# Two-stage recurrence and feed-forward block on one core: a new order of all steps, and masked copies that run along the groups

## Chip, cores and metric

The kernel runs on one core of one Trainium2 chip. The metric is device time in microseconds of one execution of the program, shown as the median of repeated runs. The core has five engines with instruction streams of their own: PE (TensorE, matrix products), DVE (VectorE), ACT (ScalarE), POOL (GpSimd) and SP (SyncE, which here only issues transfers). Each works its stream strictly in order, and waits on semaphores for the others.

## Reference

The first half is a recurrence over 768 time steps for 4 x 8 heads with a state of 40 x 40 each; the second is a gated feed-forward block on the 3072 tokens of 320 features that come out.

```python
for t in range(S):                       # r, k, v, w, a, b: (4, 8, 768, 40)
    y[:, :, t] = einsum('bhd,bhde->bhe', r_t, state)
    Sa = einsum('bhde,bhe->bhd', state, a_t)
    state = state * w_t[:, :, None, :] - einsum('bhd,bhe->bhde', Sa, b_t)
    state = state + einsum('bhd,bhe->bhde', v_t, k_t)
x = y.transpose(0, 2, 1, 3).reshape(3072, 320)
xn = x / sqrt(mean(x * x) + 1e-6) * rms_g
g = xn @ w_gate                          # 320 x 1536
out = (g * sigmoid(g) * (xn @ w_val)) @ w_out
```

All of it is float32 at the surface; the weights arrive as 64-bit floats and are narrowed on the chip.

## The kernel before

Time is cut into 24 chunks of 32 steps. For each chunk c the kernel records four stages, and for each pair of chunks a fifth:

- `front(c)` (L706) loads w, a, k, b and v of the chunk (POOL issues these transfers from the second chunk on), turns them with TensorE, and builds the strictly lower triangular matrix LT of each of the 32 heads and two halves, 32 x 32. Its entries come from products with a doubling scheme in five levels of block length 1, 2, 4, 8, 16. The innermost blocks of four steps are done at once: one set of 32 small products ("gramk", L551) of K with A gives, for each group of four columns, seven places in PSUM: three for the first diagonal below the main one (distance 1), then two for distance 2 and one that stays unused, then one for distance 3. Three masked copies, one for each distance, put them into LT. For levels 4, 8 and 16 another product and one masked copy each follow, with the mask `msk`. Between the levels VectorE and ScalarE scale and reorder K and A.
- `inverse(c)` (L810) sends LT through DRAM (sB) into the layout M, runs 31 steps of substitution on VectorE (`tmp` and `Yi`, two instructions a step), and sends the result back through DRAM (sY) into LT. SP issues these transfers.
- `main(c)` (L830) uses the inverse: solves for the chunk (X, U, written into VU), updates the state ST, forms the scores As and adds the levels to y; then normalizes and turns the tokens into xg.
- `feed(g)` (L952), after every second chunk, runs the feed-forward block on 256 tokens: 12 slices of the hidden size, whose weights come from DRAM (sW into wf, SP), with products into `ps` and `po`, silu on ScalarE (sg), a product on VectorE (hT).
- `narrow_slice(f)` (L1010) turns the 64-bit weights into float32, once, during the first feed.

The stages only record steps ("pieces"). Each piece has an engine, a time from a formula, and what it reads and writes. What comes out in the program is set by two long tables of numbers at the top of the file. ORDER names the pieces in the order in which they are issued; each engine's stream is that order restricted to its own pieces. Its numbers count from the first piece not yet issued, so that 0 is the oldest open one. A "-" in it issues one filler: a 128 x 128 product of the identity into an unused part of `po` (L1030), which keeps TensorE busy where it would have nothing to do. PAIRS names, for each of 491 uses of PSUM, which of three pairs of banks (ps0 to ps2) it takes. Both tables were written by a search outside this file that uses the pieces' time formulas; the constants S0, S1, LEAD and WARM belong to it. All pieces of one use of a PSUM pair must be done before the next use of the same pair begins.

The time formulas stand in the helpers. For VectorE (L505), a fixed part and 0.00104 us an element; for the masked copy (L519):

```python
def where(o, m, a, more=0.0):
    dve(0.08, nc.vector.copy_predicated, o, m, a, more=more)
```

so that the formula of a masked copy is 0.08 + `more` + 0.00104 for each element of a partition. The formula has no part in the program other than through the order that was searched with it. All VectorE work recorded by these helpers shows line L505 in the profile, ScalarE's copies L532 and activations L528, transfers L548, products L551, turns L554.

The names in the changed lines: LT is (128, 16, 32), a row of 32 columns for each of 16 items; `g j` splits these columns into 8 groups of 4. `near` holds three masks of 32 columns, one for each distance, the same for all items. `g4` is the PSUM result, (128, 16, 8, 7), 64 words from item to item and 7 from group to group.

Of the kernel before, what the change touches and what calls it, by code (L numbers as in the profile page):

```python
# [9 lines left out]
U32 = mybir.dt.uint32  # L10
# [6 lines left out]
P = 128  # L17
# [15 lines left out]
37 346 26 36 42 27 193 38 4 40 16 41 18 39 31 194 28 5 30 19 29 20 46 14 9 50 49 47 192 45 48 33 61 184 66 182 53 51  # L33
54 196 65 21 60 59 - 55 62 8 592 56 25 591 57 186 605 64 181 76 77 63 628 75 191 74 73 58 604 110 22 78 71 - - - - -
- - - - 67 72 602 86 70 603 23 593 34 68 84 85 626 88 82 89 183 - 79 615 594 90 97 185 616 87 83 595 345 201 6 96 32
195 596 265 43 95 11 94 202 629 388 203 35 216 197 204 597 81 99 221 400 606 598 80 391 98 617 - - - - - - - - - 91
69 599 390 208 618 187 205 209 93 399 600 619 389 108 92 601 220 206 15 101 347 620 627 12 219 109 102 214 336 215
100 188 349 210 103 398 217 651 233 397 218 44 227 211 337 387 607 225 402 621 107 226 622 7 245 1128 229 608 630
392 106 212 230 401 105 232 609 242 104 13 348 623 3 610 639 213 611 231 640 - - - - - - - - - - - - - - - - - - 222
350 631 241 228 624 632 223 239 243 253 - 234 612 240 244 238 252 407 111 633 112 237 410 408 113 613 409 114 422  # L40
614 224 235 625 115 251 249 - - - - - 246 650 250 414 236 652 116 52 411 675 1 117 199 118 263 415 412 247 198 119
256 427 120 24 641 421 416 255 121 426 189 258 264 122 439 123 962 674 420 653 10 124 424 257 200 125 423 434 664
417 973 663 126 963 127 435 128 190 129 431 261 130 425 1129 131 436 132 642 418 133 248 419 134 432 - - - - - - - -
- - - - - - - - - - - - 428 438 135 136 634 137 635 444 138 446 139 207 433 140 395 429 141 437 396 142 450 449 - -
- - - - - - 440 445 143 405 447 144 443 406 145 654 457 146 643 441 147 442 636 - 452 148 655 637 456 149 656 150
453 151 462 413 464 152 677 153 154 260 155 156 644 638 463 157 645 262 158 657 676 159 160 259 161 162 461 658 163
164 165 665 166 666 167 168 169 646 451 170 171 266 667 172 267 173 647 659 174 268 254 269 430 455 175 465 454 270
660 271 272 273 668 176 274 669 275 670 648 276 649 671 177 277 278 672 178 179 279 280 180 281 282 714 283 284 712
285 678 711 286 679 287 673 288 - - - - - - - - - - - - - - - - - - - - - - - - - - - - - - - - - - - - - - - - - -
- - - - - - - - - - - - - - - - - - - - - - - - - - - - - 338 289 680 467 290 661 469 0 339 289 466 679 337 686 290  # L50
456 711 291 340 685 292 698 293 680 660 294 681 338 699 295 682 - - - - - - - - - - 341 296 683 349 342 297 723 468
298 540 299 401 464 300 350 301 684 364 351 302 542 722 979 353 15 303 304 713 978 305 714 458 306 307 970 446 308
361 352 309 715 356 310 355 311 357 312 313 354 314 700 - - - - - - - - - - - - - 362 315 724 363 316 365 317 725
318 366 541 319 701 367 320 359 565 543 321 358 469 322 370 702 716 726 323 717 975 470 324 457 727 969 718 371 567
974 471 325 703 327 965 472 0 34 636 393 2 - - - - - - - - - 43 646 0 399 39 391 635 400 144 634 43 239 644 44 145
45 639 146 46 0 374 - - - - - - 650 429 146 375 147 46 430 148 376 654 651 400 653 652 149 377 47 150 378 657 48 151
665 3 655 656 417 152 658 391 153 669 - - - - - - 659 0 153 669 48 667 49 679 678 154 848 663 659 680 71 155 662 61
156 157 665 847 158 660 840 159 160 857 661 161 839 681 162 677 666 60 163 676 - - - - - - - - - - - - - - - - - -
670 400 849 675 164 50 440 850 165 674 1 166 858 430 0 635 380 116 391 642 640 0 116 389 380 637 117 619 349 118 620
381 387 119 661 621 120 635 382 121 - - - - - - - - - - - - - - 161 383 633 122 638 630 163 162 640 123 165 164 636  # L60
124 631 125 632 391 642 126 384 392 127 0 384 392 127 642 128 643 651 393 385 129 394 - - - - 167 653 130 395 0 521
0 515 33 36 518 0 263 0 32 37 263 610 0 39 263 0 43 520 609 521 0 40 518 0 34 298 0 37 298 0 33 514 0 34 - - - - - -
- - 41 0 36 38 0 590 47 0 41 654 42 0 293 643 0 41 293 653 0 514 - - - 41 44 293 599 642 22 498 45 653 0 514 45 2 41
642 22 599 0 433 497 514 582 0 43 442 290 581 640 44 513 291 655 650 583 514 45 292 493 0 45 655 1088 292 506 46 669
656 514 47 293 48 657 507 3 658 661 931 2 515 49 662 674 0 49 515 658 516 50 0 620 466 558 0 345 368 567 512 522 517
369 516 0 369 530 370 518 371 512 528 6 372 513 5 373 514 374 508 431 7 460 375 777 8 0 433 375 434 787 431 376 0
431 776 0 42 528 375 516 441 376 45 0 376 138 377 519 341 441 378 522 379 523 525 528 444 380 536 530 381 529 520
382 521 457 0 442 534 378 445 379 0 500 343 0 402 0 341 401 387 9 342 407 886 343 408 406 449 344 388 410 720 345
738 403 397 346 404 721 347 0 417 397 449 347 412 0 347 9 732 412 348 0 412 732 348 492 413 493 730 349 0 413 235
349 0 484 434 481 349 350 225 414 351 8 488 719 483 485 501 352 720 487 415 7 0 352 54 481 725 353 415 12 716 0 7  # L70
495 725 353 496 415 10 0 715 415 490 0 346 347 32 409 348 31 0 409 484 485 43 0 407 345 38 480 0 345 407 488 484 485
724 408 0 37 569 408 50 719 724 486 725 494 720 345 918 346 27 0 694 319 381 704 882 693 0 898 11 381 20 697 12 538
319 705 322 0 381 538 320 697 465 319 0 697 11 458 0 456 707 0 704 10 537 559 715 718 700 0 17 10 0 10 17 701 0 0
445 6 688 27 682 698 26 699 696 7 305 691 703 683 29 702 28 0 683 0 692 - - - - - - - - 685 689 31 704 708 32 540 3
44 706 687 22 300 703 686 438 2 23 700 436 0 706 700 434 696 3 714 23 41 4 32 300 701 0 692 708 39 707 19 28 293 706
703 292 29 436 37 437 20 693 50 438 0 9 684 418 419 0 682 698 419 692 420 9 488 27 0 9 420 17 489 18 421 0 487 489
490 39 697 421 38 422 9 18 0 413 0 678 - - - - - - - - - - - - 16 8 40 413 0 0 470 404 667 666 0 404 405 27 11 406 0
27 406 29 6 17 407 668 18 469 5 19 408 0 10 651 408 6 38 19 11 0 462 13 44 0 13 401 31 21 0 585 458 10 298 11 18 461
584 398 12 0 18 806 734 39 0 779 18 379 446 776 638 444 439 8 17 575 0 8 29 767 379 30 439 0 447 637 0 - 710 439 7
711 378 440 8 447 713 379 0 456 444 448 8 778 379 9 0 775 379 0 431 769 7 0 757 7 432 755 8 370 440 756 371 - - - -  # L80
- - - - 17 438 0 765 371 0 0 748 8 363 431 753 18 364 13 365 0 365 0 430 432 365 8 366 367 431 0 367 764 368 0 368 5
0 425 757 362 601 363 426 3 600 4 364 365 427 8 690 0 438 427 365 0 0 685 361 423 362 746 363 434 364 686 0 362 745
363 421 585 749 597 0 743 683 1027 745 363 421 757 762 0 363 421 773 748 364 0 421 753 0 421 363 422 2 364 747 753
365 758 3 423 366 755 4 757 367 424 594 0 747 594 367 424 369 755 368 694 766 764 4 370 765 748 0 762 764 590 591
744 0 591 756 365 592 593 594 744 421 0 756 594 595 752 795 368 432 426 753 367 596 754 366 597 761 427 767 365 428
598 769 431 599 770 764 429 773 600 601 421 602 766 603 604 605 765 422 423 768 774 606 607 776 608 609 424 433 777
610 778 785 611 612 787 434 613 690 788 614 615 786 425 436 616 1165 617 618 771 619 430 620 621 790 622 623 440 3
624 792 435 445 444 660 437 457 625 0 625 438 662 626 790 627 660 663 788 437 771 628 440 661 629 441 664 774 457
630 631 632 672 665 633 442 673 726 717 674 780 727 688 676 998 675 997 445 681 716 684 1005 634 446 635 516 636 637
683 447 638 448 639 783 640 679 452 678 677 451 641 680 642 643 682 685 453 644 795 687 449 690 695 691 645 694 692  # L90
# [333 lines left out]
def kernel(  # L424
# [42 lines left out]
    NI = 2 * N  # L467
# [51 lines left out]
    def where(o, m, a, more=0.0):  # L519
        dve(0.08, nc.vector.copy_predicated, o, m, a, more=more)  # L520
# [63 lines left out]
    near = const.tile([P, 3, C], FP32, name="near")  # L584
# [19 lines left out]
    for p0, kt, src in ((0, 0, 0), (0, 1, P), (0, 2, 2 * P), (64, 2, 2 * P)):  # L604
        m = min(P, DM - src)
# [100 lines left out]
    def front(c):  # L706
# [5 lines left out]
        for i in range(2):  # L712
# [6 lines left out]
            for x in range(2):  # L719
                at = i * 64 + x * C  # L720
# [27 lines left out]
        for dist, at in ((1, 0), (2, 3), (3, 6)):  # L748
            m = 4 - dist
# [314 lines left out]
```

## Time and profile before

| what | value |
|---|---|
| median of three runs | 1142.45 us (1137.5, 1142.45, 1143.51) |
| profiled execution | 1136.66 us |
| its span, first to last instruction | 1134.9 us |
| mean granted TensorE clock | 0.976 |
| instructions | 53027 |
| moved by DMA | 145.41 MB, mean 128 GB/s |
| instruction queue q8 | 182 packets, 2.98 MB |

The profile is one execution. PE and PEld are the two parts of TensorE's work, the products and the loads of their stationary operand; each float32 product counts as two passes, so that 275 fillers show as 550. "Idle before" a group is the time in which its engine did nothing just before an instruction of the group, with what ended it; "issue" there means that nothing in the profile explains the wait. The chain is followed from the last instruction back, at each step to what released it. By windows of 100 us, VectorE is busiest between 100 and 200 us (93.6 us of 100), TensorE from 1000 us on (128 of 135).

### The profile page before, as it was taken

The numbers are of one execution on the slowest core, as the hardware profiler recorded it, in microseconds if no ns is written. First come the engines' busy times: TensorE is split into PE (matmuls) and PEld (weight loads), VectorE is DVE, ScalarE is ACT, GpSimd is POOL, SyncE is SP. The second block draws the span as 40 slices with busy tenths as digits, with TensorE's granted clock in tenths as the row PEclk, the third lists the DMA queues.
The fourth block names the chain that finished last, engine by engine and source line by source line (L and its number), as shares of the span: only waits on it lengthen the run. The fifth ranks groups of instructions, "written<-read, shape, count | busy, mean of one in ns | idle before, by whom it ended". The sixth has DMA issues, their size and how long they took to land.

```text
span 1134.9 us, 53027 instructions
## 1 busy us (share of the span) xinstructions
PE 1036.8 (91%) x23142; PEld 853.2 (75%) x23142; DVE 864.5 (76%) x3065; ACT 437.8 (39%) x989; POOL 303.9 (27%) x534
## 2 busy tenths in 40 slices
PE   5988888889999999989998898998999999999998
PEld 4887767767777787767776687877777777777876
DVE  6998998877778789587697588887788787787421
ACT  5644455633433344234333244333334244332211
POOL 8503333221340330511422324213303402401000
PEclk8999999989999999999998999999999999999999
DMA  6645546846454453633644536455445645534342
GB/s 134 173 109 153 139 94 166 236 138 162 115 125 122 128 129 98 141 103 84 150 118 99 136 82 159 113 145 143 110 115 131 147 116 129 148 91 141 87 138 78
DMA packets 171175, 145.41 MB, mean 128 GB/s; under 512 B 123712, under 2 KB 142080, under 8 KB 170944
## 3 DMA queue, kind: packets, MB, share of 16 engines
q1 hardware_dynamic: 152576, 119.06, 38.4%
q0 software_dynamic: 16192, 22.64, 9.7%
q8 instruction: 182, 2.98, 1.1%
q10 hardware_dynamic: 2176, 0.33, 0.2%
q14 instruction: 49, 0.40, 0.1%
HBM read 125.83 MB, written 16.12 MB: 125 GB/s over the span
## 4 chain that ended last, share of the span: by engine, by line
PE 55%; DVE 19%; DMA 10%; issue 6%; SPq 4%; POOL 3%; ACT 2%; DVEq 0%; ACTq 0%; POOLq 0%
PE ps L551 37%; PE po L551 9%; PE ps L554 7%; SPq L548 4%; DVE LT L505 3%; DMA M<-sB 2%; DVE Yi L505 2%; DVE tmp L505 2%; DMA wf<-sW 2%; DVE K L505 2%; PE po L1030 1%; POOL kbn L548 1%; DMA sY<-Yi 1%; DVE Ab L505 1%; DMA sB<-LT 1%
## 5 line engine op out<-in xcount | busy, mean ns | idle before, releaser
L551 PE MATMUL ps<-xg,wf 128*128 128x256 f32 (+1 forms) x1728 | 369.2, 401 | 7.6 <-DMA wf<-sW 2.0
L551 PEld LDWEIGHTS ps<-xg,wf 128*128 128x128 f32 (+1 forms) x1728 | 264.9, 193 | 67.9 <-issue 18.6
L505 DVE TENSOR_TENSOR tmp<-Yi,M 128x60 f32<-128x60 f32 (+24 forms) x744 | 154.3, 208 | 38.0 <-DMA M<-sB 26.5
L551 PE MATMUL po<-wf,hT 128*128 128x320 f32 x576 | 178.6, 440 | 2.0 <-DVE hT L505 1.7
L505 DVE TENSOR_TENSOR Yi<-Yi,tmp 128x60 f32<-128x60 f32 (+24 forms) x744 | 153.9, 208 | 11.9
L551 PEld LDWEIGHTS po<-wf,hT 128*128 128x128 f32 x576 | 104.4, 192 | 35.1 <-DVE hT L505 3.5
L528 ACT ACTIVATE sg<-ps 128x256 f32<-128x256 f32 x144 | 53.3, 386 | 168.4 <-PE ps L551 161.5
L532 ACT COPY KN<-ps 128x640 f32<-128x640 f32 x96 | 66.3, 694 | 116.9 <-PE ps L554 46.9
L548 POOL DMA_DIRECT2D kbn<-in_k_dram x92 | 53.7, 586 | 198.0 <-PE ps L551 195.7
L505 DVE TENSOR_TENSOR hT<-ps,sg 128x256 f32<-128x256 f32 x144 | 59.2, 418 | 60.8 <-PE ps L551 35.2
L548 POOL DMA_DIRECT2D VU<-in_v_dram x92 | 53.9, 588 | 192.1 <-PE ps L554 143.4
L551 PE MATMUL ps<-Ab,K 40*64 40x56 f32 x4608 | 86.1, 221 | 17.0 <-issue 5.2
L551 PEld LDWEIGHTS ps<-Ab,K 40*64 40x64 f32 x4608 | 76.2, 135 | 33.3 <-issue 14.3
L505 DVE TENSOR_TENSOR As<-ps,msi 128x256 f32<-128x256 f32 (+1 forms) x192 | 87.7, 482 | 16.2 <-PE ps L551 15.8
L505 DVE TENSOR_TENSOR K<-K,T 128x512 f32<-128x512 f32 (+1 forms) x192 | 93.1, 489 | 6.2 <-ACT K L532 4.5
L532 ACT COPY K<-K 128x256 f32<-128x256 f32 (+1 forms) x168 | 72.1, 444 | 49.9 <-DVE K L505 31.1
L548 POOL DMA_DIRECT2D wn<-in_w_dram x92 | 52.3, 570 | 115.4 <-DVE KN L505 56.3
L548 POOL DMA_DIRECT2D kbn<-in_b_dram x92 | 53.8, 587 | 106.6 <-PE ps L551 104.8
L551 PEld LDWEIGHTS ps<-As,KN 128*40 128x40 f32 x3072 | 64.1, 122 | 17.5 <-issue 11.4
L551 PE MATMUL ps<-As,KN 128*40 128x32 f32 x3072 | 70.0, 203 | 7.2 <-issue 5.8
L1030 PE MATMUL po<-ident 128*128 128x128 f32 x550 | 72.7, 291 | 4.1 <-issue 4.1
L1030 PEld LDWEIGHTS po<-ident 128*128 128x128 f32 x550 | 68.9, 205 | 5.1 <-issue 4.1
(124 smaller groups left out, 1536.6 us busy)
## 6 DMA issues: line engine op xcount, KB each, us to landing
wf<-sW SPq DMA_DIRECT2D x144, 480.0 KB, 4.3
M<-sB SPq DMA_DIRECT2D x96, 128.0 KB, 3.5
rn<-in_r_dram SPq DMA_DIRECT2D x24, 160.0 KB, 4.6
sW<-ex SPq DMA_DIRECT2D x16, 240.0 KB, 2.6
out_dram<-o SPq DMA_DIRECT2D x48, 80.0 KB, 2.9
kbn<-in_k_dram POOLq DMA_DIRECT2D x92, 40.0 KB, 3.1
wan<-in_a_dram POOLq DMA_DIRECT2D x46, 80.0 KB, 3.6
kbn<-in_b_dram POOLq DMA_DIRECT2D x92, 40.0 KB, 2.7
```

What stands on the lines that cost most here:

```text
L505: plan.add("DVE", time + more + each * size(o), 0.087, lambda at: [fn(at(o), *m(at))], [o], aps(*args))
L528: scalar(o, [a], lambda at: nc.scalar.activation(at(o), at(a), f, **kw), aps(acc), 0.1 if f in (AF.Square, AF.Relu) else 0.0)
L532: scalar(o, [a], lambda at: nc.scalar.copy(at(o), at(a)), extra=more)
L548: plan.add(by, 0.6 if by == "POOL" else 0.45, 0.0, lambda at: queue.dma_start(out=o, in_=i), [o], [i], load=load, since=since)
L551: return o, lhsT, rhs, lambda at: nc.tensor.matmul(at(o), lhsT, rhs, start=start, stop=stop, skip_group_check=True), 4
L554: return o, i, ident, lambda at: nc.tensor.transpose(at(o), i, ident), 2
L1030: plan.warm = lambda: nc.tensor.matmul(po_[:, 0, DM:DM + P], ident, ident, start=False, stop=False, skip_group_check=True)
```

## The change

Two things change.

First, the access order of the three masked copies at L750. Before, the innermost dimension runs over the 3, 2 or 1 columns inside a group of four; after, it runs over the 8 groups, then over the 16 items, and the columns inside a group are the outermost dimension. The same elements are copied under the same mask. The extra 0.12 us in the formula goes as well.

```diff
         for dist, at in ((1, 0), (2, 3), (3, 6)):
             m = 4 - dist
-            where(LT.rearrange("p n (g j) -> p n g j", j=4)[:, :, :, dist:], near[:, dist - 1:dist].rearrange(
-                "p u (g j) -> p u g j", j=4)[:, :, :, dist:].bitcast(U32).to_broadcast((P, NI, 8, m)), g4[:, :, :, at:at + m], more=0.12)
+            by_j = lambda t: t.rearrange("p n (g j) -> p j n g", j=4)[:, dist:]
+            where(by_j(LT), by_j(near[:, dist - 1:dist]).bitcast(U32).to_broadcast((P, m, NI, 8)),
+                  g4[:, :, :, at:at + m].rearrange("p n g j -> p j n g"))
```

Second, the tables ORDER and PAIRS are replaced as a whole. The change describes this as a new search over the order of all steps, in which TensorE's instruction blocks are counted exactly; the search itself is not in the file. ORDER goes from 6546 entries with 275 fillers to 6484 with 213. The pieces are the same 6271 in both, and PAIRS has 491 digits in both.

```diff
 ORDER = """
-37 346 26 36 42 27 193 38 4 40 16 41 18 39 31 194 28 5 30 19 29 20 46 14 9 50 49 47 192 45 48 33 61 184 66 182 53 51
+26 27 37 36 33 346 194 38 183 30 11 41 18 28 40 4 31 19 29 5 39 46 14 20 48 9 50 47 186 53 182 61 54 184 51 192 22
...
 PAIRS = """
-01201202101020112210102122110120212101011000001012222100202202122122201120011012012001200011110101120102000121111011
+01210012222002220020201121110120122101011001220022211100202222100022202212000201220022101120002220012001022012220122
```

## The prediction

> **What bounds the kernel now.** I read the totals first, then the chain that ended last, then the groups with shapes kept apart, then what TensorE waits for. The page's totals and its chain (shares of the span by engine, then by line):
>
> ```profile
> PE 1036.8 (91%) x23142; PEld 853.2 (75%) x23142; DVE 864.5 (76%) x3065; ACT 437.8 (39%) x989; POOL 303.9 (27%) x534
> ...
> PE 55%; DVE 19%; DMA 10%; issue 6%; SPq 4%; POOL 3%; ACT 2%; DVEq 0%; ACTq 0%; POOLq 0%
> PE ps L551 37%; PE po L551 9%; PE ps L554 7%; SPq L548 4%; DVE LT L505 3%; DMA M<-sB 2%; DVE Yi L505 2%; DVE tmp L505 2%; DMA wf<-sW 2%; DVE K L505 2%; PE po L1030 1%; POOL kbn L548 1%; DMA sY<-Yi 1%; DVE Ab L505 1%; DMA sB<-LT 1%
> ```
>
> TensorE is the bound, with 98.1 us idle. VectorE is second, yet 19% of the chain runs over it. The masked copies into LT ("DVE LT") alone make 3%, 34 us. The whole run in stretches of 200 us (busy time of PE, PEld, DVE, ACT, POOL, each with its instructions, then the granted clock, the DMA share and GB/s):
>
> ```profile
> 0.00:200.00 200.00, 164.58 (x3964) 148.53 (x3965) 176.12 (x606) 104.91 (x217) 79.23 (x151) 0.97 0.55 139
> 200.00:400.00 200.00, 182.70 (x3832) 147.74 (x3832) 155.49 (x553) 77.68 (x173) 49.17 (x83) 0.96 0.54 144
> 800.00:1000.00 200.00, 189.60 (x4509) 153.30 (x4497) 159.26 (x570) 75.33 (x176) 56.65 (x97) 1.00 0.50 127
> ```
>
> In the first 200 us VectorE is the fuller engine (176 of 200) and TensorE idles 35 us; later TensorE idles 10 to 17 us in 200, and VectorE 40 to 48.
>
> **The masked copies: the pattern.** The groups with shapes kept apart (busy us, mean ns | idle before):
>
> ```profile
> L505 DVE COPY_PREDICATED LT<-msk,ps 128x256 f32<-128x256 uint32 x72 | 31.0, 430 | 15.2 <-PE ps L551 9.8 <-ACT KN L532 4.7
> L505 DVE COPY_PREDICATED LT<-near,ps 128x384 f32<-128x384 uint32 x24 | 17.5, 728 | 4.9 <-PE ps L551 4.1 <-DMA wf<-sW 0.4
> L505 DVE COPY_PREDICATED LT<-near,ps 128x128 f32<-128x128 uint32 x24 | 17.4, 725 | 0.2
> L505 DVE COPY_PREDICATED LT<-near,ps 128x256 f32<-128x256 uint32 x24 | 17.3, 722 | 0.1
> L505 DVE TENSOR_SCALAR ss<-ss 128x1 f32<-128x1 f32 x24 | 3.6, 150 | 23.4 <-ACT x L528 23.4
> ```
>
> The reader is to see that the three `near` copies cost the same, 0.72 us, with 384, 256 and 128 elements. So neither elements nor, it turns out, runs set the price. The built program gives the shapes: distance 1 walks 128 groups (16 items by 8) of 3 neighbouring elements, distance 2 128 groups of 2, and distance 3 has one element in each group. There the dimension of size one vanishes, so distance 3 already is 16 runs of 8 elements, 4 apart in LT and the mask and 7 apart in PSUM. That is the pattern which the change gives to distances 1 and 2, three and two times over; distance 3 stays as it is. The `msk` copies write whole groups of four, 64 of them in each of three run lengths (4, 8, 16), and cost 0.43 us. All six copies fit one rule: (725 - 430) / 64 = 4.6 ns for each visit of a group of four neighbouring words, and 0.13 us beside it. In the new order every element is a visit of its own.
>
> Priced from rows: 0.150 us for a start (the 128x1 row, the shortest here), and 0.725 - 0.150 = 0.575 us for a block of 128 such elements. Distance 1 becomes 0.150 + 3 x 0.575 = 1.875 us, distance 2 1.300, distance 3 0.725: 3.900 in place of 2.175, +1.725 a chunk, x 24 chunks = +41.4 us of VectorE. Bounds: below, a copy that contains the distance 3 block can't be cheaper than it, so 3 x 0.725 = 2.175, and nothing is gained; above, each block pays its start again, 4.350, +52.2 us in all. I take 41.4, since one instruction starts once.
>
> The Trainium skill bears on it (page "SBUF — State Buffer", section "Door 1: The DMA port swizzle (why `[64,N]` ≈ `[32,N]`)"): SBUF lines are 16 bytes, two or more consecutive hits in a line run at full rate, and an access that crosses to a new line pays. It speaks against the change, as the row does. By its two-hit clause distances 1 and 2 would be at full rate now, an estimate of 0.55 and 0.42 us, and the change would cost 53 us; the rows show them at 0.72 already.
>
> **How much of it reaches the end.** On VectorE, in order, the next elements of the inverse (tmp, Yi), the scaling of K and Ab, the copies to VU and hT stand behind these copies, and TensorE waits for VU, hT and K; the PSUM pair of the product is freed by the third copy. One chunk of the chain, in order of time (start, us, what):
>
> ```profile
> 612.92 6.09 PE ps L551 x87
> ...
> 619.03 0.74 DVE LT L505
> 619.77 0.02 issue
> 619.79 0.74 DVE LT L505
> 620.54 0.02 issue
> 620.56 0.73 DVE LT L505
> ...
> 624.28 0.42 DVE hT L505
> ...
> 624.85 1.05 PE ps L554 x8
> ```
>
> From 619 to 625 us the path is VectorE's, the three copies first; TensorE resumes 0.2 us late. Longer copies push that out one for one. Adding up the pieces of the chain that lie in the `near` copies, 25.4 of their 52.2 us (0.49) are on it. Where they are off it, VectorE's idle time has to take up 1.7 us; summing its gaps after each such copy in the trace, that takes 10 to 30 us in most chunks, and all work in between is late. So between 0.49 x 41.4 = 20 and 41 us arrive; I take 0.65, 27 us. The last of these copies starts at 999 us, so the last 135 us have none.
>
> **The new order.** Instruction counts are the same on every engine but for 62 fewer fillers (L1030, 275 to 213, each two passes). The transfers are as many as before (712 on SP, 460 on POOL, 8 on ACT), in another sequence on each queue; the placing by stage hardly moves: of the 24 first products of a chunk none stands more than 32 TensorE instructions from its old place, the first feed still follows 1295 real products, and the `near` copies move by at most some ten places on VectorE. It is a reshuffle within stages.
>
> ```profile
> L1030 PE MATMUL po<-ident 128*128 128x128 f32 x550 | 72.7, 291 | 4.1 <-issue 4.1
> ...
> PEld ps L551 <- issue: 80.8, 143, 3.0
> ...
> PE ps L551 <- issue: 33.2, 32, 2.8
> ```
>
> 550 passes cover 72.7 us, so 124 fewer leave 16.4 us of cover; 40 of the 62 go before the first feed. If the new order fills that time with real products, 16.4 us are gained; if they were only cover for waits, nothing. Below nothing too: the code's own charge for the three copies falls from 1.40 to 1.04 us a chunk (its formulas at L519), while I expect 3.90, so work is placed for results that come 2.9 us late where it was 0.8 before; I allow 5 us of loss. I take 8 gained. Counting the instruction blocks removes few of them: 124 passes with their loads are 248 of 46,284 instructions, about one of the 182 refills on the page's instruction queue. Fewer fillers could lower the clock: 0.01 less over TensorE's 165 busy us in the first 200 is 1.6 us; I take 0, as it stands at 0.97. The moved transfers: DMA and SP's queue hold 14% of the chain (159 us); a twentieth either way is 8 us, taken as 0.
>
> The skill's "Runtime: NRT & Kernel Launch", section "Instruction fetch mechanics", says that crossing a block is mostly hidden; by it, knowing the blocks exactly would be worth nothing. The rows show 33 us of TensorE idle with no other releaser.
>
> **Sum.** The profiled execution took 1136.66 us (span 1134.9 plus 1.8). 1136.7 + 27 - 8 = 1155.7. It lies 5.8 us below the median of 1142.45, in a spread of 6, so I add 2.3: 1158.
>
> **Rivals.**
> Copies as the short runs would suggest: the `msk` copies with runs of 8 take 0.43 us for 256 elements, so 0.57, 0.43 and 0.29, a saving of 0.885 a chunk, 21 us; half on the chain, 10, with 8 from the order: 1119 to 1121. For it: that one row. Against: distance 3, already in runs of 8, at 0.725. It decides if a new distance 1 copy takes under 0.73 us. Chance 0.08.
> The order's gain cancels the copies: 20 us arrive and 16.4 are gained, 1140 to 1146. For it: TensorE's 35 idle us and the fillers at the start. Against: places hardly move. Chance 0.22; I count 0.06 of it faster, 0.13 the same, 0.03 slower.
> Everything arrives: 41 us and nothing gained, 1178 to 1180; with 52, 1190. For it: VectorE at 88% in the first 200 us and the long way to its next idle time. Against: the 51% off the chain. Chance 0.18.
> The forecast: 20 to 35 us arrive and 0 to 12 are gained, 1147 to 1174. Chance 0.52.
>
> **How the numbers follow.** A measurement here tells 0.5%, 5.7 us, from no change. Faster 0.08 + 0.06 = 0.14, same 0.13, slower 0.52 + 0.18 + 0.03 = 0.73. The range runs from the cancelling case to full arrival of 41.4 with the clock's loss, 1139 to 1182: it leaves out the cheap copies, part of the cancelling case and the dearest end, about 0.18.
>
> **What would show it.** The `near` rows after: 1.88, 1.30 and 0.73 us, VectorE busy about 906 us; "DVE LT" at 5% or more of the chain; idle of TensorE behind VectorE's results up by some 20 us; 426 filler passes. Wrong if distances 1 and 2 stay at 0.73 or below, or if TensorE's idle time stays at 98 us with 41 us more on VectorE.

## The result, and the profile after

The change makes the kernel slower: 1201.26 us median (1198.82 to 1203.89, 4 runs) against 1142.98 us (1137.5 to 1146.8, 4 runs), a ratio of 1.0514 with a 95% interval from 1.0462 to 1.0566. The direction and the price of the copies were as predicted, the size was not: 58 us where 16 were forecast, and above the range. The profiled execution took 1198.82 us, its span is 1197.0 us.

The page's totals and its chain, after (helpers' line numbers are three lower than before, since the tables are shorter):

```profile
PE 1059.5 (89%) x23018; PEld 866.6 (72%) x23018; DVE 912.1 (76%) x3065; ACT 438.5 (37%) x989; POOL 302.2 (25%) x534
...
PE 50%; DVE 26%; DMA 10%; issue 4%; SPq 4%; ACT 2%; POOL 2%; DVEq 0%; ACTq 0%; POOLq 0%
PE ps L548 32%; PE po L548 9%; PE ps L551 7%; DVE LT L502 7%; SPq L545 4%; DVE Yi L502 3%; DVE tmp L502 3%; DMA M<-sB 3%; DVE K L502 2%; DMA wf<-in_moe_w_val_dram 2%; DVE y L502 2%; DMA kbn<-in_k_dram 1%; PE po L1028 1%; DMA sB<-LT 1%; POOL kbn L545 1%
```

VectorE's share of the chain went from 19% to 26%, and the copies into LT from 3% to 7%. Two lines hold the surprise. TensorE has 124 passes fewer and is busy 22.7 us longer; and its idle time is 137.5 us, up by 39.4. The two make the 62.1 us by which the span grew. The masked copies, with shapes kept apart (busy us, mean ns | idle before):

```profile
L502 DVE COPY_PREDICATED LT<-near,ps 128x384 f32<-128x384 uint32 x24 | 44.9, 1872 | 7.1 <-issue 3.6 <-PE ps L548 3.3
L502 DVE COPY_PREDICATED LT<-msk,ps 128x256 f32<-128x256 uint32 x72 | 31.0, 431 | 16.2 <-PE ps L548 12.6 <-ACT KN L529 2.7
L502 DVE COPY_PREDICATED LT<-near,ps 128x256 f32<-128x256 uint32 x24 | 30.9, 1287 | 0.1
L502 DVE COPY_PREDICATED LT<-near,ps 128x128 f32<-128x128 uint32 x24 | 17.2, 718 | 0.2
```

1.87, 1.29 and 0.72 us, 93.1 us in all against 52.2. The kernel in stretches of 200 us (columns as before):

```profile
0.00:200.00 200.00, 153.81 (x3346) 137.90 (x3347) 169.29 (x545) 89.97 (x183) 74.82 (x147) 0.85 0.47 117
200.00:400.00 200.00, 178.83 (x3738) 141.98 (x3740) 160.74 (x523) 82.06 (x181) 41.56 (x70) 0.93 0.55 147
800.00:1000.00 200.00, 178.68 (x4134) 145.63 (x4132) 154.09 (x526) 70.91 (x167) 58.16 (x99) 0.95 0.48 124
```

The column after the brackets of POOL is the granted clock: 0.85, 0.93 and 0.95 where it was 0.97, 0.96 and 1.00. Over the span it fell from 0.976 to 0.939. The records of the clock know full and half speed only, so the time at half speed is twice the missing share: 2 x 0.024 x 1134.9 = 55 us before, 2 x 0.061 x 1197.0 = 146 us after (147 when the records are added up, as in the table below). That is the first place to look for the rest. The second is what TensorE waited for (us in total, times, longest), here the waits for VectorE and the unexplained ones, and the fillers:

```profile
PE ps L548 <- DVE tmp L502: 18.8, 7, 4.6
PE ps L548 <- DVE LT L502: 18.7, 10, 4.8
PE ps L548 <- DVE Yi L502: 11.3, 6, 2.3
PE ps L548 <- issue: 10.8, 12, 1.9
...
L1028 PE MATMUL po<-ident 128*128 128x128 f32 x426 | 61.8, 307 | 2.5 <-ACT o L529 2.5
```

The first three were 2.3, 2.6 and 3.8 us before. The unexplained waits fell from 33.2 to 10.8 us. That is a gain, and it belongs to the new order: with the old copies it has 11.9 us of them too, while the old order with the new copies has 36.6 (runs e1 and e2 below).

### The profile page after: what moved, and what is told of

Same layout as the page of the kernel before. It is cut to its first block, busy times and chain, and to the rows that moved or that the text cites. A ratio compares the mean times of both kernels' runs of the same rounds, so it can differ in the third digit from the quotient of the medians.

```text
span 1197.0 us, 52790 instructions
## 1 busy us (share of the span) xinstructions
PE 1059.5 (89%) x23018; PEld 866.6 (72%) x23018; DVE 912.1 (76%) x3065; ACT 438.5 (37%) x989; POOL 302.2 (25%) x534
## 3 DMA queue, kind: packets, MB, share of 16 engines
q1 hardware_dynamic: 152576, 119.06, 36.6%
## 4 chain that ended last, share of the span: by engine, by line
PE 50%; DVE 26%; DMA 10%; issue 4%; SPq 4%; ACT 2%; POOL 2%; DVEq 0%; ACTq 0%; POOLq 0%
PE ps L548 32%; PE po L548 9%; PE ps L551 7%; DVE LT L502 7%; SPq L545 4%; DVE Yi L502 3%; DVE tmp L502 3%; DMA M<-sB 3%; DVE K L502 2%; DMA wf<-in_moe_w_val_dram 2%; DVE y L502 2%; DMA kbn<-in_k_dram 1%; PE po L1028 1%; DMA sB<-LT 1%; POOL kbn L545 1%
## 5 line engine op out<-in xcount | busy, mean ns | idle before, releaser
L548 PE MATMUL ps<-xg,wf 128*128 128x256 f32 (+1 forms) x1728 | 380.1, 410 | 10.2 <-DVE tmp L502 3.7
L548 PEld LDWEIGHTS ps<-xg,wf 128*128 128x128 f32 (+1 forms) x1728 | 274.4, 199 | 71.1 <-issue 16.0
L502 DVE TENSOR_TENSOR tmp<-Yi,M 128x60 f32<-128x60 f32 (+24 forms) x744 | 159.0, 214 | 43.2 <-DMA M<-sB 21.7
L548 PE MATMUL po<-wf,hT 128*128 128x320 f32 x576 | 185.3, 452 | 3.4 <-DVE hT L502 2.2
L502 DVE TENSOR_TENSOR Yi<-Yi,tmp 128x60 f32<-128x60 f32 (+24 forms) x744 | 156.4, 211 | 13.6 <-DVE tmp L502 0.2
L548 PEld LDWEIGHTS po<-wf,hT 128*128 128x128 f32 x576 | 107.3, 198 | 37.6 <-issue 5.0
L548 PE MATMUL ps<-Ab,K 40*64 40x56 f32 x4608 | 88.8, 229 | 50.6 <-DVE LT L502 15.6
L548 PEld LDWEIGHTS ps<-Ab,K 40*64 40x64 f32 x4608 | 79.5, 142 | 70.9 <-issue 22.3
L529 ACT COPY K<-K 128x256 f32<-128x256 f32 (+1 forms) x168 | 73.0, 444 | 74.0 <-DVE K L502 41.4
L502 DVE COPY_PREDICATED LT<-near,ps 128x384 f32<-128x384 uint32 (+2 forms) x72 | 93.1, 1293 | 7.4 <-issue 3.6
L1028 PE MATMUL po<-ident 128*128 128x128 f32 x426 | 61.8, 307 | 2.5 <-ACT o L529 2.5
```

Of the source, the lines that this page charges most:

```text
L502: plan.add("DVE", time + more + each * size(o), 0.087, lambda at: [fn(at(o), *m(at))], [o], aps(*args))
L529: scalar(o, [a], lambda at: nc.scalar.copy(at(o), at(a)), extra=more)
L548: return o, lhsT, rhs, lambda at: nc.tensor.matmul(at(o), lhsT, rhs, start=start, stop=stop, skip_group_check=True), 4
L1028: plan.warm = lambda: nc.tensor.matmul(po_[:, 0, DM:DM + P], ident, ident, start=False, stop=False, skip_group_check=True)
```

## Experiments

All ratios are to the kernel before, run on the same chip. 0.01 is 11.4 us. In the table, "near" is VectorE's time in the three copies, "half" the time at half clock (from the granted clock of the profiled execution), "idle" what TensorE's busy time leaves of the span, and "unexpl." the part of TensorE's waits that nothing in the profile explains (the rows `PE ... <- issue`, added up). All four come from one profiled execution of each kernel.

| kernel | ratio (95% interval) | near us | idle us | half us | unexpl. us |
|---|---|---|---|---|---|
| before | 1 | 52 | 98 | 55 | 38 |
| after | 1.0514 (1.0462 to 1.0566) | 93 | 137 | 147 | 15 |
| after, once more (h0) | 1.0461 (1.0402 to 1.0520) | 93 | 143 | 154 | 15 |
| e1 new order, old copies | 0.9920 (0.9886 to 0.9954) | 52 | 106 | 59 | 15 |
| e2 old order, new copies | 1.0381 (1.0331 to 1.0430) | 93 | 134 | 107 | 39 |
| e3 before, 62 fillers less | 0.9956 (0.9920 to 0.9992) | 52 | 111 | 72 | 43 |
| e4 after, 62 fillers more | 1.0433 (1.0374 to 1.0492) | 93 | 134 | 106 | 11 |
| h2 new order, distance 2 alone new | 1.0038 (1.0004 to 1.0072) | 66 | 123 | 82 | 19 |
| f4 new order, distance 1 alone new | 1.0242 (1.0180 to 1.0303) | 80 | 129 | 120 | 12 |
| f3 new order, old copies twice | 1.0688 (1.0624 to 1.0752) | 104 | 161 | 168 | 15 |
| f1 after, 287 fillers in its waits | 1.0393 (1.0328 to 1.0458) | 94 | 104 | 69 | 33 |
| h1 after, 156 fillers in its waits | 1.0410 (1.0358 to 1.0462) | 93 | 117 | 102 | 34 |
| f2 e1 with 152 fillers in its waits | 0.9979 (0.9944 to 1.0014) | 52 | 100 | 22 | 28 |
| g5 e1, distance 1 as a product | 0.9903 (0.9866 to 0.9939) | 35 + 13 | 110 | 80 | 12 |
| h3 g5 with 98 fillers in its waits | 0.9984 (0.9949 to 1.0019) | 35 + 13 | 92 | 75 | 34 |
| i1 g5 with 107 of 213 fillers | 1.0138 (1.0089 to 1.0188) | 35 + 13 | 128 | 144 | 36 |
| i2 g5 without fillers | 1.0046 (1.0012 to 1.0081) | 35 + 13 | 154 | 151 | 34 |

**The two parts apart.** e1 is the kernel before with ORDER and PAIRS of after; e2 is after with the tables of before.

```diff
 e1 (against after)
-            by_j = lambda t: t.rearrange("p n (g j) -> p j n g", j=4)[:, dist:]
-            where(by_j(LT), ...
+            where(LT.rearrange("p n (g j) -> p n g j", j=4)[:, :, :, dist:], ...
 e2 (against after)
-ORDER = """ 26 27 37 36 33 346 ...
+ORDER = """ 37 346 26 36 42 27 ...
```

> New ORDER and PAIRS, copies as before. Theory A (the copies cost it nearly all: 41 us more on VectorE, some waits of TensorE that follow, and half-clock stretches that those waits bring): 1130 to 1147 us, TensorE clock 0.97 or more, some 14 half-clock stretches. Theory B (the new order itself is bad on the chip, and costs the 20 us beyond the 41): 1158 to 1170. Theory C (the copies arrive one to one and the 62 missing fillers cost the rest through the clock): 1150 to 1165 with a clock of 0.95 to 0.96 in the first 230 us.

> Old ORDER and PAIRS, copies as after the change. Theory A: 1190 to 1210 us, granted clock about 0.94, near 30 half-clock stretches. Theory B: 1142 + 20 to 41 = 1162 to 1184. Theory C: 1165 to 1184, clock 0.96 or more, since the fillers are there.

The order alone gains 0.8%, 9 us. The copies alone cost the old order 3.8%, 44 us, and the new one 62 us (1.0461 - 0.9920) to 68 us (1.0514 - 0.9920). So theory B falls: the new order is good by itself. It is also the one that bears the longer copies worse.

**The fillers that the new order lacks.** e3 takes 62 fillers out of the old list, evenly; e4 puts 62 into the new one, each beside one that is there.

> The kernel before with 62 of its 275 fillers left out, evenly over the list. Theory A and B: 1140 to 1148 us, the fillers cover waits. Theory C: 1155 to 1165 with more half-clock stretches in the first 230 us.

> The kernel after with 62 fillers added beside its own 213, evenly. Theory A and B: 1195 to 1215 us, as after or somewhat slower. Theory C: 1180 to 1190, clock in the first 230 us back from 0.85 to 0.95.

e3 came out a little faster than before, so the smaller number does no harm by itself, and theory C falls. In e4 the half-clock time fell from 147 to 106 us and the time did not follow (1.0433, inside the interval of h0, the same kernel as after).

The last column of the table tells more. In the trace of before, 34 of the 35 unexplained waits stand at one place in 256 of TensorE's stream (counted from 0, the instructions after them are the 193rd to 195th), and the instruction queue q8 has 182 packets for the 46,607 TensorE instructions of the trace, one for 256. So these waits come with the instruction blocks, as it seems at their borders. The old order has 38 to 43 us of them, whatever its copies and fillers (before, e2, e3); the new order with its own 213 fillers has 12 to 19, in all ten kernels that have it so. A filler is four instructions, so fillers that are added or left out move all that follows against the borders: in the six kernels below that change their number in the new order it is 28 to 36 us again. e4 has 11; its 62 fillers move the stream by 248 instructions, nearly a whole block.

**How much time for how much copying.** With the new order the added VectorE time was set to four sizes.

```diff
 f4: distance 1 as after, 2 and 3 as before (h2: "dist == 2")
+            if dist == 1:
                 where(by_j(LT), ...
+            else:
+                where(LT.rearrange("p n (g j) -> p n g j", j=4)[:, :, :, dist:], ...
 f3: old pattern, each near copy issued twice
-        dve(0.08, nc.vector.copy_predicated, o, m, a, more=more)
+        plan.add("DVE", ..., lambda at: [nc.vector.copy_predicated(at(o), at(m), at(a)) for _ in range(times)], ...)
```

> New order, only distance 2 in the new pattern, +0.57 us a chunk, 13.7 us in all. On a straight line from nothing through the 27.5 us of distance 1 (1.024 against 0.992): ratio 1.008. With slack that swallows the first part: 0.992 to 1.000.

> New order; the copy of distance 1 as after, distances 2 and 3 as before: +1.15 us a chunk in place of +1.71, 27.5 us in all. If the cost follows the added time in a straight line: 1139 + 62 x 0.67 = 1180. If a first part is swallowed by slack: 1160 to 1172.

> New order, old copies, each of the three near copies issued twice in a row: 2.18 us a chunk more on VectorE, 52 us in all, with the old access pattern. Theory A (only the time on VectorE counts): 1139 + 52 x 1.5 = 1205 to 1225, near 30 half-clock stretches. Theory D (the new access pattern also slows others, through the memories): less than 1195, since the pattern is the old one.

> The kernel after once more, beside the others on one chip: 1.043 to 1.052 of before, to set the size of what the copies cost in the new order.

Against e1: 13.6 us more on VectorE cost 13 us, 27.5 cost 37, 41 cost 62 to 68, 52 cost 88. There is no slack at the start, and the cost of an added microsecond rises from 1.0 (0.6 to 1.4 by the intervals) to 1.7. The doubled old copies fit the same curve, so what counts is the time that VectorE spends, not the pattern as such; theory D falls.

**Which operand makes the pattern dear.** Three variants of after, one execution each, each with one operand of the copies made contiguous over the 8 groups and 16 items (g1: the mask, g2: the PSUM side, by storing A with the groups innermost, g3: the written side, so that the diagonals land in wrong places of LT).

```diff
 g1  near[:, dist] written through .rearrange("p (j g) -> p g j", j=4), read back in that order
 g2  A_ = Turns(1, [P, NI, 7, 8], "A", whole)    # was [P, NI, 8, 7]
 g3
-            where(by_j(LT), ...
+            where(LT.rearrange("p n c -> p (n c)").rearrange("p (j n g) -> p j n g", j=4, n=NI)[:, dist:], ...
```

> The kernel after, with the mask of each distance stored with the 8 groups next to each other, so that the mask is read in runs of 8 neighbouring words; LT and PSUM stay strided. If the 4.5 ns an element belong to the mask's read: copies of 0.55, 0.42 and 0.28 us for distances 1, 2, 3 (0.15 + 1.04 ns an element). If they belong to another operand: 1.87, 1.29, 0.72 as after.

> The kernel after, with the product's seven columns stored so that the 8 groups of one column lie next to each other in PSUM (A is stored that way too); LT and mask stay strided. If the price belongs to the PSUM read: 0.55, 0.42, 0.28 us. If not: 1.87, 1.29, 0.72.

> The kernel after, with the three copies writing LT in a block of neighbouring words, so that the three diagonals land elsewhere in LT; mask and PSUM stay strided. If the price belongs to the write: 0.55, 0.42, 0.28 us. If not: 1.87, 1.29, 0.72. If it is a sum over operands, all three of these runs fall by a part.

With the mask contiguous the copies took 1867, 1284 and 717 ns, with PSUM contiguous 1875, 1290 and 717: nothing. With the write contiguous (the groups with shapes apart, of g3):

```profile
L502 DVE COPY_PREDICATED LT<-near,ps 128x384 f32<-128x384 uint32 x24 | 20.1, 839 | 7.9 <-issue 3.9 <-PE ps L548 3.7
L502 DVE COPY_PREDICATED LT<-near,ps 128x256 f32<-128x256 uint32 x24 | 14.5, 605 | 0.1
...
L502 DVE COPY_PREDICATED LT<-near,ps 128x128 f32<-128x128 uint32 x24 | 9.0, 374 | 0.2
```

So it is the write: 1.8 ns an element with a contiguous write, where the strided reads remain, against 4.5 ns with the strided one. A masked copy that writes in this pattern pays for each visit of a group of four words. The one execution of g3 took 1129.96 us, with 44 us of near copies where e1 has 52.

**A version with less of it.** A product with the mask writes every element and was a candidate for not paying that price. It can replace the first copy alone, because what it sets to zero is zero or is written later.

```diff
+            if dist == 1:
+                tt(lt, g4[:, :, :, at:at + m], nr.to_broadcast((P, NI, 8, m)), MUL)
+            else:
                 where(lt, nr.bitcast(U32).to_broadcast((P, NI, 8, m)), g4[:, :, :, at:at + m], more=0.12)
```

> New order, old copies for distances 2 and 3; distance 1 as a product with the mask (it is the first to write, and what it sets to zero is zero or is written later). If an ordinary product doesn't pay the visits: 0.15 + 384 x 1.04 to 1.56 ns = 0.55 to 0.75 us in place of 0.73, so 0 to 4 us less on VectorE and 1133 to 1139 against 1139 for the new order alone. If it pays them like the masked copy: no change.

```profile
L502 DVE TENSOR_TENSOR LT<-ps,near 128x384 f32<-128x384 f32 x24 | 13.3, 553 | 5.8 <-PE ps L548 3.0 <-issue 2.5
```

0.553 us = 0.150 + 384 x 1.05 ns: an ordinary product into the same runs of three shows no price for its visits. The 4 us saved don't stand out of the measurement beside e1, but 0.9903 (0.9866 to 0.9939) is better than both kernels.

**The clock.** Where does the part beyond one to one come from? One place, the same instructions in two kernels. First e1, the timeline from the first masked copy on (start, us, engine, instruction, and in brackets the idle time before it with its releaser), then the same stretch after the change:

```profile
321.06 0.73 DVE L502 COPY_PREDICATED LT<-near,ps 128x384 f32<-128x384 uint32 x1 [3.37 <-issue]
...
323.19 1.49 DVE L502 COPY_PREDICATED LT<-near,ps 128x256 f32<-128x256 uint32 x2
...
324.73 1.15 PE L548 MATMUL ps<-Ab,K 40*64 40x56 f32 x64 [0.93 <-DVE tmp L502]
...
325.81 2.86 PE L548 MATMUL ps<-xg,wf 128*128 128x256 f32 x12
```

```profile
332.82 1.88 DVE L502 COPY_PREDICATED LT<-near,ps 128x384 f32<-128x384 uint32 x1 [3.46 <-issue]
...
336.07 2.03 DVE L502 COPY_PREDICATED LT<-near,ps 128x256 f32<-128x256 uint32 x2
...
338.16 1.16 PE L548 MATMUL ps<-Ab,K 40*64 40x56 f32 x64 [2.61 <-DVE tmp L502]
...
339.24 4.54 PE L548 MATMUL ps<-xg,wf 128*128 128x256 f32 x12
```

The copies are 1.7 us longer. TensorE's wait grows by the same, from 0.93 to 2.61 us: one to one. Then the same 12 products take 4.54 us and not 2.86. From the first copy to their end it is 7.6 us in e1 and 11.0 after: 3.35 us for 1.7. The stretches around it, e1 and then after:

```profile
324.70:334.70 10.00, 9.97 (x279) 8.12 (x279) 8.59 (x33) 5.46 (x14) 0.58 (x1) 1.00 0.03 7
```

```profile
338.00:348.00 10.00, 9.84 (x224) 8.08 (x225) 7.20 (x27) 5.35 (x13) 0.58 (x1) 0.83 0.01 2
```

The granted clock is 1.00 in the one, 0.83 in the other: 3.4 of the 10 us at half speed. Counting all waits of TensorE (products and loads together) in ten of the traces (before, after, e1, e2, f3, f4, g5, h0, h2, i1), from 60 us on, that began at full clock, and whether a half-clock stretch began within 7 us after the wait's start:

```
wait of TensorE     followed by half clock     not followed
0.5 to 1.0 us             47                       238
1.0 to 1.5                31                        75
1.5 to 2.0                41                        41
2.0 to 2.5                51                        12
2.5 to 3.0                28                         8
3.0 to 4.0                31                         6
```

A wait under 1 us is followed by half clock once in six, which is little more than chance (a half-clock stretch begins within 7 us of one moment in seven at full clock), one of 2 us or more four times in five. In e1 TensorE waits for more than a microsecond 23 times, after 46 times. Since the stretches last 3.4 us or a multiple, each 3.4 us cost up to 1.7 us of TensorE's work. It fits the bend of the curve above, where a small dose leaves most waits short.

The rest of the scatter comes from where a wait falls. In each of the twenty traces the clock changes only at the points of a fixed grid of 3.413 us. Counted by these windows (at full clock, from 60 us on), what tells is TensorE's idle time within the window just over: 2 us or more in all was followed by half clock 170 times in 171, 1.25 to 2 us 159 times in 342, under 0.75 us 5 times in 5025. A wait of 2 us that lies across a point of the grid can pass.

That the clock is what makes TensorE's work longer shows in the ten kernels with the new order and its own 213 fillers, which run the same 23,018 passes in the same order: busy time and half-clock time lie on one line, 0.43 us more for each microsecond at half clock, none off it by more than 3 us (e1 1022 us at 59, h2 1030 at 82, f4 1052 at 120, after 1060 at 147, f3 1068 at 168, the last with the old access pattern).

Can the clock be held by fillers in these waits? f1 puts 287 into the 47 places of after with a wait of a microsecond or more (counted at the products alone), f2 152 into e1's 24 places, each a little shorter than its wait; h1 and h3 put in half as much.

```diff
 ORDER of f1, ahead of the product that waited 2.61 us (h1: four)
+- - - - - - - -
```

> The kernel after, with 287 more fillers, put just ahead of the 47 places where its profile shows TensorE idle for a microsecond or more, each time a little less than the gap holds. Theory A1 (what goes beyond 41 us is TensorE at half clock after those waits): half-clock time falls from 147 us towards 50, the time from 1201 to 1170 to 1185. Theory A2 (the clock is only a by-product of waiting, the work that counts runs on VectorE): half-clock time falls, and the time stays at 1195 to 1205.

> New order, old copies, with 152 more fillers ahead of the 24 waits of a microsecond or more in that kernel's profile. Theory A1: half-clock time from 59 to 25 us, time from 1139 to 1125 to 1133. Theory A2: 1136 to 1143, no change.

> The kernel after with 156 more fillers in its waits of a microsecond or more, half as long as each wait, so that they delay nothing themselves (41 us of fillers in 108 us of waits). Theory A1 (the half clock after a wait is on the path): half-clock time from 147 to under 90 us and the time down by about half of what is saved, 15 to 30 us, a ratio of 1.02 to 1.035. Theory A2 (the clock is a by-product): half-clock time down, ratio 1.043 to 1.052.

> The kernel with the product for distance 1 and 98 more fillers in its waits, half as long as each wait. Theory A1: half-clock time from 80 to 50 us, ratio 0.978 to 0.985. Theory A2: 0.987 to 0.994.

The half-clock time fell each time, in f1 from 147 to 69 us, but the time gave only some 6 to 14 us in f1 and h1, and f2 and h3 became slower. The fillers were not free. The 156 of h1 hold TensorE for 41 us, and half of the 52 us less at half clock is 26, so its busy time rose by 16. Its idle time fell by 25 and not by 41: 19 us of unexplained waits came back (33.7 against 14.7 in h0), since the fillers move the stream against the block borders. 16 - 25 is about the 10 us by which the two spans differ (1207.1 and 1197.3). In f1, f2 and h3 17, 13 and 22 us of these waits came back. So these runs don't separate the clock from the borders; neither theory's numbers were met.

i1 and i2 go the other way and take fillers out of g5, so that the fillers' own work can't be to blame; the borders move here too.

```diff
 ORDER of g5 (i1: every second "-" left out; i2: all of them)
-59 60 - 55 49 66 21 591
+59 60 55 49 66 21 591
```

> The kernel with the product for distance 1, every second of its 213 fillers left out. If fillers cost TensorE about what they save in clock (as adding them did): 0.985 to 0.995, as with all of them (0.990). If the half clock is on the path: half-clock time from 80 to over 110 us and a ratio above 1.000.

> The same with none of the 213 fillers (56 us of TensorE work less). If they pay for themselves alone: 0.985 to 0.995. If the half clock is on the path: half-clock time above 130 us, ratio 1.01 or more.

The unexplained waits of g5 and then i1 (us in total, times, longest):

```profile
PE ps L548 <- issue: 10.4, 11, 2.0
PE ps L551 <- issue: 1.8, 2, 1.7
```

```profile
PE ps L543 <- issue: 29.8, 33, 2.7
PE ps L546 <- issue: 3.8, 3, 2.5
PE po L543 <- issue: 2.3, 1, 2.3
```

i1 has some 28 us less of fillers (212 passes at the 0.13 us of before) and takes 2.35% longer than g5, 27 us, with half-clock time up from 80 to 144 us; its granted clock is 0.77 in the first 200 us against 0.91. TensorE is busy 6 us longer with 28 us less to do, which is the clock. It is idle 18 us longer, and there the unexplained waits grew by 24 us. Leaving work out made the kernel slower, through both; how much of the 27 us either would cost alone, i1 doesn't show. i2, without any, has about the same half-clock time and unexplained waits and is 10 us faster than i1; that i1's fillers ran mostly at half clock (42.2 us for 214 passes, 0.20 us each) and were of little use would fit, but it wasn't tested.

## Why the prediction was right or wrong

- **Price of the copies: right.** 1.875, 1.300 and 0.725 us were forecast, 1.872, 1.287 and 0.718 measured; +41.4 us against 93.1 - 52.2 = 40.9, VectorE 912 us busy against 906. That distance 3 already ran in the new pattern gave the price. g3 adds that the write alone is dear. The rule of the Trainium skill that the prediction weighed ("SBUF — State Buffer", section "Door 1: The DMA port swizzle (why `[64,N]` ≈ `[32,N]`)") pointed the right way; its two-hit clause didn't hold for this write (0.728 us with three hits in a line, 0.725 with one).
- **The new order: right in size, in part by luck.** 8 us of gain were taken, e1 shows 9. They were taken for the fillers' time, and e3, the old order with as few fillers, does have some 5 of them (0.9956); knowing the blocks was taken to be worth about one refill. The number of refills did fall by one (182 to 181), but the waits at the borders fell from 38 to 15 us. Of that gain part went again to waits for VectorE: 19 us in e1 for `tmp`, LT and `Yi`, 9 before. The fear of 5 us lost through misjudged costs was not separate: the order loses by them only together with the longer copies, and then more (62 to 68 us against 44).
- **"So between 0.49 x 41.4 = 20 and 41 us arrive; I take 0.65, 27 us": wrong, and this decides.** The share on the chain was read from a chain in which the copies were short; after, 78 of 93 us of them lie on it, as the pieces of the chain inside the copies add up. In both orders nearly every added microsecond became idle time of TensorE: +36 us in the old order, +32 to 37 in the new. The upper bound was wrong too. "Longer copies push that out one for one" takes the time of TensorE's own work as fixed, and it is not.
- **"Fewer fillers could lower the clock ... I take 0": the missing term.** The clock was priced for the fillers alone, not for the waits that the copies would lengthen. Half-clock time rose by 52 us in the old order and by 88 to 95 in the new (from e1), and TensorE's busy time by 24 and 37 to 42 us at the same work. With idle time of 32 to 37 us and busy time of 37 to 42 the new order's 69 to 79 us of span are whole; that the whole 37 to 42 would come back if the clock alone were held is not shown. The difference of the two orders, some 18 to 24 us by the ratios, is about half the difference of their half-clock time (the profiled execution of e2 was the slowest of its six, so by the profiles the orders differ less); why the new order falls to half clock more often was not tried.
- **Rivals.** "Everything arrives" (1178 to 1190) had the mechanism and 0.18; 1201 lies above it by the clock. Cheap copies and a cancelling order are out: 1.87 us, and 1.0381 with the old order.
- **Signs named ahead.** The three rows, "DVE LT" above 5% of the chain (7%) and 426 passes came; idle time rose by 39 us in place of 20.

Put together again from measured rows: 1136.7 - 9 + 35 (idle) + 39 (TensorE at half clock) = 1202. The last two terms are read from the result, so the sum shows what the terms should have been and tests nothing.

## What to carry to other kernels

Before a pattern is rewritten, look for an instruction in the trace that already has it: a dimension of size one vanishes, and the last of three copies was the experiment. Where the bound engine's clock depends on its being fed, an added wait can't be priced at one to one: ask how long the wait becomes, and whether that length brings the slower clock. A filler put in or left out moves all instructions behind it, so look at the waits that nothing explains before its effect is put down to the clock. And an order tuned closely to assumed costs should be tried apart from the change of costs: the order alone was worth 0.8%, and it was hidden behind a loss of 6%.

## What was not expected of the hardware

- A masked copy on VectorE pays about 4.5 ns for each visit of a group of four words that it writes, whether it writes 1, 2 or 3 of them (0.72 us for 128 visits). With a contiguous write and strided mask and PSUM reads an element still takes 1.8 ns, where the `msk` copies take 1.1 ((431 - 150) / 256); that the strided reads make this difference wasn't tried alone. A product into the same places shows no price for visits (0.553 us for 384 elements).
- Waits of TensorE of 2.0 to 2.5 us were followed by half clock 51 times in 63. The Trainium skill ("TensorE: Matmul & The Clock Gate", section "HAM oscillation — how this bites in real kernels") gives idle gaps of more than about 3.4 us as what to avoid. Here shorter ones did it, and the stretches of 3.4 us and its multiples agree with the window that the page describes. What counted was the sum of the idle time in one window of the grid: 2 us or more brought half clock 170 times in 171.
- TensorE's unexplained waits come at one place in 256 instructions (34 of 35 before). The new order has 12 to 19 us of them, the old one 38 to 43, and fillers that move the new order's stream against the blocks bring back 28 to 36.
